# Layer one's first product of the first tile in four parts

## The chip, the cores and the metric

The kernel runs on one core of one Trainium2 chip. Five engines work side by side, each through its own list of instructions in order: TensorE (PE, with its weight loads as PEld), VectorE (DVE), ScalarE (ACT), GpSimd (POOL) and SyncE (SP), which starts the transfers that 16 DMA engines carry out. The metric is device time in microseconds (us), the median of three runs.

## The reference

Attention over 4 batches, 8 heads, 576 positions and 64 values per head; the first four heads see a window of 32 keys, the others every fourth key of a window of 128. Its output, 2304 rows of 512, goes through two layers.

```
scores = scale * np.matmul(q, k.transpose(0, 1, 3, 2))       # masked, softmax, times v
x = attn_out.transpose(0, 2, 1, 3).reshape(B * S, H * D)     # 2304 x 512

h = x @ w_in                                                 # layer one: 512 -> 1024
e = np.exp(h - np.max(h, axis=-1, keepdims=True))
solu = h * e / (np.sum(e, axis=-1, keepdims=True) + 1e-09)
ln = (solu - mean) / np.sqrt(var + 1e-06) * g_ln
y = ln @ w_out                                               # 1024 -> 512

h = y @ w2_in                                                # layer two: 512 -> 2048
out = (h * (1.0 / (1.0 + np.exp(-1.702 * h)))) @ w2_out      # 2048 -> 512
```

## The kernel before

**Three stages.** In the first some 280 us attention and layer one run interleaved, then layer two runs over three passes of 768 rows. A matmul of layer one takes each operand as a high and a low part: `x @ w` is `xh wh + xh wl + xl wh`.

**Attention units.** Each batch has five units: units 0 to 3 hold a pair of heads each with its first 512 queries, unit 4 the last 64 queries of all heads. A unit is a chain: scores on TensorE (tile `s`, line 271, after a mask that is added on TensorE at 267), row maximum on VectorE (`mx`, 306), exponential on ScalarE (`t`, 324 one window at a time, or 333 after VectorE's subtraction at 314), sums and reciprocal on VectorE (`sx`, 339 to 341), normalising on GpSimd or VectorE (346), transposition on TensorE (`ptp`, 354), copy (`pt`, 360), product with the values on TensorE (`xt`, 384 or 387: 64 matmuls in the trace), and two copies into the ring of rows `xr` (402, 406). `HPS = [0, 2, 1, 3]` says which pair of heads, and so which 128 of the 512 columns of a row (`kt`), a unit fills: units 1 and 3 fill columns `kt` 2 and 3, units 0 and 2 fill 0 and 1.

**Layer one.** A tile is 128 rows. `moe_xh` copies them from `xr` to `xh`, `moe_xl` makes `xl`, `moe_h` multiplies by one half of the 1024 columns of `w_in`: 4 `kt` by 3 products, 12 matmuls for a half, 24 for a tile.

**Weights.** `w_in` comes in four chunks as 64 bit words: chunk `c` holds `kt` 2(c mod 2) and the next, of the column half c // 2. Each is turned into float by two shifts (432 on ScalarE; 440 on ScalarE or 436 on VectorE), joined on VectorE (444), and split into `wi_h` (481) and `wi_l` (494).

**What sets the order.** Every step is a "work" with an engine. `ORDER`, a table of work numbers, gives the order in which all engines' instructions are written, `PICKS` the engine of the works that may run on several. Each engine runs its list in order and waits by semaphores for its operands and for free buffers. Where the planner's own reckoning shows a gap ahead of a TensorE work, `stir` writes up to four filler matmuls (line 253), which compute nothing that is used.

Of the kernel before, what the change touches and what calls it, by code (L numbers as in the profile page):

```python
# [9 lines left out]
F32R = mybir.dt.float32r  # L10
# [5 lines left out]
ALU = mybir.AluOpType  # L16
AX = mybir.AxisListType

P = 128
B, H, S, D = 4, 8, 576, 64  # L20
NT, DM, FF1, FF2 = 2304, 512, 1024, 2048
KT = DM // P
# [7 lines left out]
RING = 2 * S  # L30
# [135 lines left out]
def attention_moe_kernel(ctx, tc, qk, qk_last, v, v_last, masks, w_in, w_out, g_ln, w2_in, w2_out, out):  # L166
    nc = tc.nc
# [3 lines left out]
    def f32(ap):  # L171
        return ap.bitcast(F32)
# [332 lines left out]
    def moe_xh(i, copy):  # L505
        c0 = (i * P) % RING
        xh = hp_.tile([P, KT, P], F32R, tag="xh", bufs=2, name=f"xh{i}")
        copy(xh, xr[:, :, c0:c0 + P])
        xs[i] = [xh]

    def moe_xl(i, eng=nc.gpsimd):
        c0 = (i * P) % RING
        xl = hp_.tile([P, KT, P], F32R, tag="xl", bufs=2, name=f"xl{i}")
        eng.tensor_tensor(xl, xr[:, :, c0:c0 + P], f32(xs[i][0]), ALU.subtract)
        xs[i].append(xl)

    def moe_h(i, half):
        if half == 0:
            hps[i] = psA.tile([P, 2, 512], F32, tag="A", name=f"h{i}")
        stir(hps[i][:, half, :])  # L520
        xh, xl = xs[i]
        fs = slice(half * 512, half * 512 + 512)
        for kt in range(KT):
            for j, (x, w) in enumerate(((xh, wi_h), (xh, wi_l), (xl, wi_h))):
                nc.tensor.matmul(hps[i][:, half, :], x[:, kt, :], w[:, kt, fs],  # L525
                                 start=(kt == 0 and j == 0), stop=(kt == KT - 1 and j == 2))
# [422 lines left out]
    for i in range(NTILE):  # L949
# [5 lines left out]
        xh = add(r, "ACT", 0.63, lambda i=i: moe_xh(i, nc.scalar.copy), units, take=("x",), pick=0, port=True,  # L955
                 also=[("DVE", 0.42, lambda i=i: moe_xh(i, nc.vector.tensor_copy)),
                       ("POOL", 1.1, lambda i=i: moe_xh(i, nc.gpsimd.tensor_copy))])
        xl = add(r, "POOL", 1.3, lambda i=i: moe_xl(i), [xh], port=True,
                 also=[("DVE", 0.75, lambda i=i: moe_xl(i, nc.vector))] if i in XL_ANY else [])
        h0 = add(r, "PE", 2.8, lambda i=i: moe_h(i, 0), [xh, xl] + [w[c] for c in range(2) for w in (hi, lo)], take=("A",))  # L960
        h1 = add(r, "PE", 2.8, lambda i=i: moe_h(i, 1), [h0] + [w[c] for c in range(2, 4) for w in (hi, lo)], give=("x",))
# [324 lines left out]
def plan_sequence():  # L1286
# [29 lines left out]
    for b in range(1, B):  # L1316
        todo, k = items[b - 1], 0
        for u in range(UB):
# [30 lines left out]
XL_ANY = (0,)  # L1349
LO_POOL = (2,)  # L1350
# [15 lines left out]
ORDER = [1, 8, 56, 57, 58, 59, 18, 87, 88, 89, 0, 46, 60, 61, 4, 9, 77, 47, 48, 90, 49, 62, 50, 51, 78, 10, 97, 52, 7,  # L1366
# [243 lines left out]
```

## Time and profile before

| | |
|---|---|
| median of 3 runs | 651.91 us (651.39 to 652.36) |
| profiled execution | 652.14 us, span 650.4 us, mean granted clock 0.99 |
| TensorE busy | 631.7 us, 97% of the span, 5596 matmuls |
| VectorE, ScalarE, GpSimd busy | 436.1, 344.8, 265.7 us |
| moved by DMA | 163.53 MB, 251 GB/s in the mean |

The times come from one execution with a profiler. An engine's busy time over the span tells how much of the span it could be the limit; where it idles, the trace names what it waited for. A granted clock of 1 is TensorE's full 2.4 GHz, 0.5 is 1.2 GHz.

### The profile page before, as it was taken

How to read it: one execution, taken by the hardware profiler on the slowest of the kernel's cores; microseconds unless marked ns; L12 is line 12 of the kernel's file. 1: busy time of each engine (PE TensorE's matmuls, PEld its weight loads, DVE VectorE, ACT ScalarE, POOL GpSimd, SP SyncE). 2: the span in 40 equal slices, each digit the busy share in tenths (PEclk: the TensorE clock that was granted, in tenths of full speed). 3: DMA queues.
4: the chain of work that ended last, by engine and by line, in shares of the span. 5: the costliest groups of instructions: out<-in, count | busy, mean ns of one | idle time of the engine just before them, and what ended most of it. 6: DMA issues, size and time to landing. Idle time of an engine off the chain costs nothing.

```text
span 650.4 us, 14261 instructions
## 1 busy us (share of the span) xinstructions
PE 631.7 (97%) x5596; PEld 592.6 (91%) x5596; DVE 436.1 (67%) x773; ACT 344.8 (53%) x737; POOL 265.7 (41%) x331
## 2 busy tenths in 40 slices
PE   7599999999999999999999999999999999999997
PEld 4377888888989898999999999999999999999997
DVE  4689888475687566585778979433566854246784
ACT  4668976376444664754555765223265532235652
POOL 1317655836556766744365031202432340232232
PEclk9779999999999999999999999999999999999999
DMA  8959646643457547956999989776798957778783
GB/s 330 406 209 354 220 133 212 228 151 125 154 182 225 188 149 254 360 179 187 324 338 358 350 280 365 241 254 223 272 293 268 347 177 256 267 268 283 251 266 130
DMA packets 65011, 163.53 MB, mean 251 GB/s; under 512 B 6960, under 2 KB 28592, under 8 KB 64944
## 3 DMA queue, kind: packets, MB, share of 16 engines
q1 hardware_dynamic: 64944, 162.62, 73.4%
q8 instruction: 44, 0.72, 0.4%
q14 instruction: 23, 0.19, 0.1%
HBM read 126.42 MB, written 36.18 MB: 250 GB/s over the span
## 4 chain that ended last, share of the span: by engine, by line
PE 88%; DMA 7%; DVE 3%; POOL 1%; issue 1%; ACT 0%; SPq 0%; POOLq 0%; DVEq 0%; ACTq 0%
PE hz L720 15%; PE oz L798 15%; PE y L599 14%; PE h L525 14%; PE hx L720 12%; PE ox L798 11%; DMA w_t<-in_w_in_dram 3%; PE lt L579 2%; PE xt L387 1%; DMA wo<-wdo 1%; PE xt L384 1%; DMA y_early<-in_w_in_dram 1%; PE s L271 1%; DMA wdq<-park_hl 1%; PE ptp L354 1%; DMA qk<-in_qk_dram 1%
## 5 line engine op out<-in xcount | busy, mean ns | idle before, releaser
L763 ACT CAST gs<-g 128x384 fp32r<-128x384 f32 x168 | 84.1, 512 | 76.3 <-DVE g L759 27.3
L766 POOL TENSOR_TENSOR gs<-g,gs 128x384 fp32r<-128x384 f32 x47 | 49.9, 1067 | 144.1 <-ACT gs L763 136.0
L720 PE MATMUL hz<-yc,ws 128*128 128x384 f32 x492 | 98.5, 334 | 0.0
L599 PE MATMUL y<-ln_t,wo_h 128*128 128x384 f32 x384 | 98.5, 337 | 0.0
L766 DVE TENSOR_TENSOR gs<-g,gs 128x384 fp32r<-128x384 f32 x121 | 68.7, 590 | 28.1 <-ACT gs L763 26.3
L720 PEld LDWEIGHTS hz<-yc,ws 128*128 128x128 f32 x492 | 86.5, 188 | 0.0
L720 PE MATMUL hx<-yc,ws 128*128 128x384 f32 x369 | 74.7, 335 | 0.0
L599 PEld LDWEIGHTS y<-ln_t,wo_h 128*128 128x128 f32 x384 | 68.9, 188 | 0.5
L720 PEld LDWEIGHTS hx<-yc,ws 128*128 128x128 f32 x369 | 64.9, 188 | 0.0
L599 PE MATMUL y<-ln_t,wo_l 128*128 128x384 f32 x192 | 64.3, 335 | 0.0
L525 PE MATMUL h<-wi_h,xh 128*128 128x512 f32 x144 | 59.1, 410 | 0.5 <-DVE t L314 0.5
L798 PE MATMUL ox<-gs,wo 128*128 128x384 f32 x288 | 55.3, 337 | 1.4 <-DMA wo<-wdo 1.3
L525 PE MATMUL h<-wi_h,xl 128*128 128x512 f32 x144 | 56.5, 392 | 0.0
L525 PE MATMUL h<-wi_l,xh 128*128 128x512 f32 x144 | 56.3, 391 | 0.0
L798 PE MATMUL oz<-gs,wo 128*128 128x384 f32 x288 | 54.7, 336 | 0.0
L749 ACT ACTIVATE g<-g 128x384 f32<-128x384 f32 x72 | 36.4, 521 | 34.1 <-DVE g L742 13.1
L798 PE MATMUL oz<-gs,w 128*128 128x384 f32 x288 | 53.2, 337 | 0.0
L798 PEld LDWEIGHTS ox<-gs,wo 128*128 128x128 f32 x288 | 50.2, 188 | 2.2 <-DMA wo<-wdo 1.6
L798 PEld LDWEIGHTS oz<-gs,w 128*128 128x128 f32 x288 | 50.2, 188 | 0.4 <-DVE gs L766 0.4
L798 PEld LDWEIGHTS oz<-gs,wo 128*128 128x128 f32 x288 | 50.3, 188 | 0.1
L759 POOL TENSOR_TENSOR g<-g,g 128x384 f32<-128x384 f32 x21 | 22.8, 1089 | 66.4 <-ACT g L749 24.8
L759 DVE TENSOR_TENSOR g<-g,g 128x384 f32<-128x384 f32 x75 | 43.6, 597 | 7.6 <-POOL gs L766 5.8
(412 smaller groups left out, 1196.7 us busy)
## 6 DMA issues: line engine op xcount, KB each, us to landing
wo<-wdo SPq DMA_DIRECT2D x48, 512.0 KB, 6.0
ws<-wdq SPq DMA_DIRECT2D x41, 512.0 KB, 5.7
w<-wdo SPq DMA_DIRECT2D x72, 256.0 KB, 5.4
ws<-wdq SPq DMA_DIRECT2D x41, 384.0 KB, 4.8
qk<-in_qk_dram SPq DMA_DIRECT2D x14, 528.0 KB, 6.9
v<-in_v_dram SPq DMA_DIRECT2D x14, 512.0 KB, 6.8
out_dram<-ob SPq DMA_DIRECT2D x11, 384.0 KB, 5.9
w_t<-in_w_in_dram SPq DMA_DIRECT2D x8, 512.0 KB, 9.2
```

The lines of the kernel that those rows point to most:

```text
L271: nc.tensor.matmul(ps[QB * j:QB * j + QB, h, m * KW:m * KW + KW], q_[rows, c:c + QB], k_[rows, c:c + KW], start=not masked, stop=not maske ...
L354: nc.tensor.transpose(ps[:, j * P:j * P + P], t[:, 2 * j:2 * j + 2, :].rearrange("p m k -> p (m k)"), ident)
L384: nc.tensor.matmul(o, w, pt[rows, x:x + QB].rearrange("p (r t) -> p r t", r=4), start=True, stop=True, tile_position=(64 * par, 64 * h))
L525: nc.tensor.matmul(hps[i][:, half, :], x[:, kt, :], w[:, kt, fs], start=(kt == 0 and j == 0), stop=(kt == KT - 1 and j == 2))
L579: nc.tensor.transpose(ps[:, j, :], es[i][:, f * P:f * P + P], ident)
L599: nc.tensor.matmul(yps[g, dm][:, 0:TG].rearrange("p (t n) -> p t n", t=GT), w[:, f, ds_], x[:, :, f, :], start=(f == 0 and j == 0), stop=( ...
L720: nc.tensor.matmul(ps[:, 0:TB2], quad_weights(p, q, m, kk, a), yc2[m][:, x, kk, :], start=(m < 4 and kk == 0 and i == 0), stop=(kk == 1 an ...
L749: nc.scalar.activation(g_tile(q, 0, 0) if (half, b) == (0, 0) else src, src, AF.Gelu_apprx_sigmoid)
L759: eng.tensor_tensor(o_block(jj, *o), o_block(jj, *x), o_block(jj, *y_), op)
L763: nc.scalar.copy(gsp[jj, m][:, 0], o_block(jj, half, b))
L766: eng.tensor_tensor(gsp[jj, m][:, 1], o_block(jj, half, b), f32(gsp[jj, m][:, 0]), ALU.subtract)
L798: nc.tensor.matmul(ps, w, gsp[jj, m][:, x], start=m < 4 and first and i == 0, stop=last and i == 2, skip_group_check=True)
```

## The change

The product of tile 0 (`H_PARTS`) is made in four works in place of two: for `kt` 2 and 3 both column halves, then for `kt` 0 and 1 both column halves (`H_KTS`). Each has its own half of `xh` and `xl`, and waits for the two attention units and the one weight chunk that it reads in place of all four units and two chunks. The bank is opened by the first part (`start`) and closed by the last (`stop`). With the parts of `xh` and `xl` these are eight works in place of four, so the table has 2411 numbers in place of 2407, and the tables `ORDER` and `PICKS` are made anew for the whole program.

```diff
+    def moe_xh(i, copy, kts=range(KT)):
+        c0, k = (i * P) % RING, slice(kts[0], kts[-1] + 1)
+        if i not in xs:
+            xs[i] = [hp_.tile([P, KT, P], F32R, tag=f"x{z}", bufs=2, name=f"x{z}{i}") for z in "hl"]
+        copy(xs[i][0][:, k], xr[:, k, c0:c0 + P])
...
+    def moe_h(i, half, kts=range(KT)):
+        if i not in hps:
             hps[i] = psA.tile([P, 2, 512], F32, tag="A", name=f"h{i}")
-        stir(hps[i][:, half, :])
+        first, last = (0, KT - 1) if len(kts) == KT else (H_KTS[0][0], H_KTS[1][-1])
+        if kts[0] == first:
+            stir(hps[i][:, half, :])
...
-        for kt in range(KT):
+        for kt in kts:
             for j, (x, w) in enumerate(((xh, wi_h), (xh, wi_l), (xl, wi_h))):
                 nc.tensor.matmul(hps[i][:, half, :], x[:, kt, :], w[:, kt, fs],
-                                 start=(kt == 0 and j == 0), stop=(kt == KT - 1 and j == 2))
+                                 start=(kt == first and j == 0), stop=(kt == last and j == 2))
...
+        parts = H_KTS if i in H_PARTS else ()
+        for z, kts in enumerate(parts):
+            xh = add(r, "ACT", 0.38, lambda i=i, k=kts: moe_xh(i, nc.scalar.copy, k),
+                     [u for u, hp in zip(units, HPS) if hp in kts] + [xl], take=("x",)[z:], pick=0, port=True,
...
+            h0 = add(r, "PE", 1.4, lambda i=i, k=kts: moe_h(i, 0, k),
+                     [xl] + [w[kts[0] // 2] for w in (hi, lo)] + ([h0] if z else []), take=("A",)[z:])
+            h1 = add(r, "PE", 1.4, lambda i=i, k=kts: moe_h(i, 1, k),
+                     [h0] + [w[2 + kts[0] // 2] for w in (hi, lo)] + ([h1] if z else []), give=("x",)[:z])
...
+H_PARTS = (0,)
+H_KTS = ((2, 3), (0, 1))
...
-ORDER = [1, 8, 56, 57, 58, 59, 18, 87, 88, 89, 0, 46, 60, 61, 4, 9, 77, 47, 48, 90, 49, 62, 50, 51, 78, 10, 97, 52, 7,
```

TensorE, the start of tile 0's product, before: behind the transposition of unit 4 and the scores of unit 6 of the next batch (`s_646`) come 12 matmuls of the first column half (`h_695`), of which the first four rows and the last stand here.

```order
L354 MATMUL ptp_639<-ident,t_200 128x128 x2
...
L271 MATMUL s_646<-qk_597 32x64 x32
L253 LDWEIGHTS ident_b
L253 MATMUL h_695<-ident_b 128x512
L525 MATMUL h_695<-wi_h,xh_685 128x512
L525 MATMUL h_695<-wi_l,xh_685 128x512
...
L525 MATMUL h_695<-wi_h,xl_689 128x512
L384 MATMUL xt_0_725<-pt_691,vl_129 64x4x8
```

The same place in the changed program: unit 0's values product (`xt_0_592`), the transposition of unit 4, two fillers, 12 matmuls (six for each column half), then the values of unit 2 (`xt_0_687`).

```order
L384 MATMUL xt_1_593<-pt_457,v_476 64x4x8
L354 MATMUL ptp_633<-ident,t_247 128x128 x2
L253 LDWEIGHTS ident_b
L253 MATMUL h_652<-ident_b 128x512
...
L525 MATMUL h_652<-wi_h,xh_630 128x512
L525 MATMUL h_652<-wi_l,xh_630 128x512
...
L525 MATMUL h_652<-wi_h,xl_631 128x512
L253 LDWEIGHTS ident_b
L253 MATMUL xt_0_687<-ident_b 128x512
```

The product's first 12 matmuls now stand ahead of the values product of the fourth unit, and the other 12 behind it, a transposition, a score unit and unit 4's values.

VectorE around the rows' split of tile 0, before:

```order
L444 SCALAR_TENSOR_TENSOR w_t<-w_t 128x1024
L481 CAST wi_h<-w_t 128x2x512
L494 TENSOR_TENSOR wi_l<-w_t,wi_h 128x2x512 x2
L508 CAST xh_685<-xr 128x512
L514 TENSOR_TENSOR xl_689<-xr,xh_685 128x512
L306 TENSOR_REDUCE mx_693<-s_646 128x8
```

And in the changed program, from the low part of the second chunk to the last one:

```order
L494 TENSOR_TENSOR wi_l<-w_t,wi_h 128x2x512
L509 CAST xh_630<-xr 128x256
L306 TENSOR_REDUCE mx_636<-s_478 128x8
L513 TENSOR_TENSOR xl_631<-xr,xh_630 128x256
L436 TENSOR_SCALAR w_t<-w_t 128x1024
L444 SCALAR_TENSOR_TENSOR w_t<-w_t 128x1024
...
L444 SCALAR_TENSOR_TENSOR w_t<-w_t 128x1024 x2
L494 TENSOR_TENSOR wi_l<-w_t,wi_h 128x2x512
L513 TENSOR_TENSOR xl_631<-xr,xh_630 128x256
L494 TENSOR_TENSOR wi_l<-w_t,wi_h 128x2x512
```

The rows are split in two halves of 256 columns, with the conversion of the last two weight chunks between the halves. `s_478` is a score unit of the next batch.

SP, the loads of weights and values after the second weight chunk, before (`w_t` are chunks, two transfers each):

```order
L234 DMA y_early<-in_v_dram 128x1024
L425 DMA w_t<-in_w_in_dram 128x1024 x2
L234 DMA y_early<-in_v_dram 128x1024
L234 DMA v_530<-in_v_dram 128x1024
L425 DMA w_t<-in_w_in_dram 128x1024 x2
```

And in the changed program:

```order
L228 DMA qk_451<-in_qk_dram 128x1056
L234 DMA v_462<-in_v_dram 128x1024
L234 DMA v_476<-in_v_dram 128x1024
L425 DMA w_t<-in_w_in_dram 128x1024 x4
L425 DMA w_t<-in_w_out_dram 128x1024 x2
L234 DMA y_early<-in_v_dram 128x1024
```

The last two chunks of `w_in` now stand together, with the first chunk of `w_out` behind them and the values of one unit (`y_early`) behind that.

## Rows read from the trace of the kernel before

**Rows 1.** The page's engine line: busy us, share of the span, instructions.

```profile
PE 631.7 (97%) x5596; PEld 592.6 (91%) x5596; DVE 436.1 (67%) x773; ACT 344.8 (53%) x737; POOL 265.7 (41%) x331
```

**Rows 2.** Windows: us, busy of each engine, clock, DMA share, GB/s.

```profile
10.00:20.00 10.00, 5.19 (x178) 3.50 (x176) 6.87 (x15) 6.87 (x21) 1.35 (x2) 0.95 1.03 401
20.00:30.00 10.00, 7.49 (x173) 4.96 (x173) 5.28 (x10) 5.31 (x16) 2.70 (x2) 0.71 1.02 409
30.00:40.00 10.00, 8.00 (x206) 6.12 (x207) 7.87 (x13) 6.42 (x10) 2.08 (x2) 0.66 0.41 159
...
300.00:400.00 100.00, 98.58 (x567) 97.96 (x566) 80.32 (x151) 58.35 (x119) 35.54 (x42) 1.00 0.92 319
```

**Rows 3.** Timeline of TensorE from 0 to 36 us: start, us, engine, line, operation.

```profile
12.68 0.35 PE L271 MATMUL s<-y_early 64*32 64x64 f32 x16 [1.60 <-issue]
...
21.04 1.08 PE L384 MATMUL xt<-pt,v 64*64 64x32 f32 x31 [3.81 <-issue]
...
22.05 1.89 PE L253 MATMUL ptp<-ident_b 128*128 128x512 bf16 x4
...
27.28 0.88 PE L387 MATMUL xt<-pt,y_early 64*64 64x32 f32 x42 [0.60 <-issue]
...
31.43 0.66 PE L354 MATMUL ptp<-ident,t 128*128 128x128 f32 x4 [2.29 <-POOL t L346]
...
32.87 1.93 PE L384 MATMUL xt<-pt,y_early 64*64 64x32 f32 x64 [0.57 <-DVE pt L360]
```

**Rows 4.** Windows of TensorE between the ends of its stops.

```profile
12.60:21.00 8.40, 4.11 (x127) 0.88 1.03 406
21.00:27.20 6.20, 5.64 (x127) 0.61 1.03 408
```

**Rows 5.** DMA from 0 to 60 us: the queue of instructions; packets, MB, share.

```profile
q8 instruction: 8, 0.13, 0.8%
```

**Rows 6.** Timeline of TensorE from 39 to 54 us.

```profile
39.79 0.58 PE L525 MATMUL h<-wi_h,xh 128*128 128x512 f32 x1
...
44.53 0.50 PE L525 MATMUL h<-wi_h,xh 128*128 128x512 f32 x1
...
47.15 0.39 PE L525 MATMUL h<-wi_h,xl 128*128 128x512 f32 x1
...
47.70 0.86 PE L271 MATMUL s<-qk 64*32 64x64 f32 x64
...
48.49 1.09 PE L354 MATMUL ptp<-ident,t 128*128 128x128 f32 x8
...
50.76 0.47 PE L525 MATMUL h<-wi_h,xh 128*128 128x512 f32 x1 [0.49 <-DVE t L314]
```

**Rows 7.** Timeline of VectorE from 0 to 62 us.

```profile
32.73 1.22 DVE L444 SCALAR_TENSOR_TENSOR w_t<-w_t 128x1024 uint32<-128x1024 uint32 x1
...
34.71 2.36 DVE L494 TENSOR_TENSOR wi_l<-w_t,wi_h 128x1024 fp32r<-128x1024 f32 x2
36.98 0.42 DVE L508 CAST xh<-xr 128x512 fp32r<-128x512 f32 x1
37.44 0.69 DVE L514 TENSOR_TENSOR xl<-xr,xh 128x512 fp32r<-128x512 f32 x1
```

**Rows 8.** Timeline of ScalarE from 0 to 62 us.

```profile
10.90 1.75 ACT L324 ACTIVATE t<-s,mx 128x64 f32<-128x64 f32 x8
```

**Rows 9.** Chain of waits from 360 to 380 us: start, us, what.

```profile
369.64 7.84 DMA wo<-wdo
```

**Rows 10.** Windows of TensorE around the changes of its clock.

```profile
18.00:20.00 2.00, 0.00 (x0) 0.76 1.06 402
25.00:26.00 1.00, 1.00 (x66) 0.56 0.98 389
30.00:32.00 2.00, 0.57 (x5) 1.00 1.03 409
39.00:40.00 1.00, 1.00 (x66) 0.74 0.00 0
```

More of the change, by code (lines that the diff above doesn't have):

```diff
@@ L503, in attention_moe_kernel, with moe_xl @@
     lns, hps, es, xs, stat, sums = {}, {}, {}, {}, {}, {}
[L505 to L518, printed above, removed]
+    def moe_xh(i, copy, kts=range(KT)):
[3 more added lines that the diff above has]
+        copy(xs[i][0][:, k], xr[:, k, c0:c0 + P])
+    def moe_xl(i, eng=nc.gpsimd, kts=range(KT)):
+        c0, k = (i * P) % RING, slice(kts[0], kts[-1] + 1)
+        eng.tensor_tensor(xs[i][1][:, k], xr[:, k, c0:c0 + P], f32(xs[i][0][:, k]), ALU.subtract)
+    def moe_h(i, half, kts=range(KT)):
+        if i not in hps:
             hps[i] = psA.tile([P, 2, 512], F32, tag="A", name=f"h{i}")
-        stir(hps[i][:, half, :])
+        first, last = (0, KT - 1) if len(kts) == KT else (H_KTS[0][0], H_KTS[1][-1])
+        if kts[0] == first:
+            stir(hps[i][:, half, :])
         xh, xl = xs[i]
         fs = slice(half * 512, half * 512 + 512)
-        for kt in range(KT):
+        for kt in kts:
             for j, (x, w) in enumerate(((xh, wi_h), (xh, wi_l), (xl, wi_h))):
                 nc.tensor.matmul(hps[i][:, half, :], x[:, kt, :], w[:, kt, fs],
-                                 start=(kt == 0 and j == 0), stop=(kt == KT - 1 and j == 2))
+                                 start=(kt == first and j == 0), stop=(kt == last and j == 2))
     def h_flat(i):
@@ L954, in attention_moe_kernel @@
         r = at["h", i]
-        xh = add(r, "ACT", 0.63, lambda i=i: moe_xh(i, nc.scalar.copy), units, take=("x",), pick=0, port=True,
+        parts = H_KTS if i in H_PARTS else ()
+        xl = None
+        for z, kts in enumerate(parts):
+            xh = add(r, "ACT", 0.38, lambda i=i, k=kts: moe_xh(i, nc.scalar.copy, k),
+                     [u for u, hp in zip(units, HPS) if hp in kts] + [xl], take=("x",)[z:], pick=0, port=True,
+                     also=[("DVE", 0.29, lambda i=i, k=kts: moe_xh(i, nc.vector.tensor_copy, k)),
+                           ("POOL", 0.5, lambda i=i, k=kts: moe_xh(i, nc.gpsimd.tensor_copy, k))])
+            xl = add(r, "POOL", 0.75, lambda i=i, k=kts: moe_xl(i, nc.gpsimd, k), [xh], port=True,
+                     also=[("DVE", 0.42, lambda i=i, k=kts: moe_xl(i, nc.vector, k))])
+            h0 = add(r, "PE", 1.4, lambda i=i, k=kts: moe_h(i, 0, k),
+                     [xl] + [w[kts[0] // 2] for w in (hi, lo)] + ([h0] if z else []), take=("A",)[z:])
+            h1 = add(r, "PE", 1.4, lambda i=i, k=kts: moe_h(i, 1, k),
+                     [h0] + [w[2 + kts[0] // 2] for w in (hi, lo)] + ([h1] if z else []), give=("x",)[:z])
+        if parts:
+            h_of[i], xh_of[i] = h1, xl
+        xh = parts or add(r, "ACT", 0.63, lambda i=i: moe_xh(i, nc.scalar.copy), units, take=("x",), pick=0, port=True,
                  also=[("DVE", 0.42, lambda i=i: moe_xh(i, nc.vector.tensor_copy)),
                        ("POOL", 1.1, lambda i=i: moe_xh(i, nc.gpsimd.tensor_copy))])
-        xl = add(r, "POOL", 1.3, lambda i=i: moe_xl(i), [xh], port=True,
+        xl = xl or add(r, "POOL", 1.3, lambda i=i: moe_xl(i), [xh], port=True,
                  also=[("DVE", 0.75, lambda i=i: moe_xl(i, nc.vector))] if i in XL_ANY else [])
-        h0 = add(r, "PE", 2.8, lambda i=i: moe_h(i, 0), [xh, xl] + [w[c] for c in range(2) for w in (hi, lo)], take=("A",))
-        h1 = add(r, "PE", 2.8, lambda i=i: moe_h(i, 1), [h0] + [w[c] for c in range(2, 4) for w in (hi, lo)], give=("x",))
+        h0 = parts or add(r, "PE", 2.8, lambda i=i: moe_h(i, 0), [xh, xl] + [w[c] for c in range(2) for w in (hi, lo)], take=("A",))
+        h1 = h1 if parts else add(r, "PE", 2.8, lambda i=i: moe_h(i, 1), [h0] + [w[c] for c in range(2, 4) for w in (hi, lo)], give=("x",))
         h_of[i], xh_of[i] = h1, xl
@@ L1365 @@
 ULO_ANY = True
-ORDER = [1, 8, 56, 57, 58, 59, 18, 87, 88, 89, 0, 46, 60, 61, 4, 9, 77, 47, 48, 90, 49, 62, 50, 51, 78, 10, 97, 52, 7,
[123 rows of a table removed]
-PICKS = {50: 1, 52: 1, 54: 1, 55: 1, 73: 1, 86: 1, 91: 1, 104: 1, 127: 1, 136: 1, 146: 1, 159: 1, 160: 1, 168: 1,
[20 rows of a table removed]
+ORDER = [1, 4, 77, 78, 79, 18, 87, 88, 89, 0, 46, 47, 48, 80, 90, 8, 9, 267, 56, 266, 81, 82, 49, 50, 57, 58, 83, 59,
[123 rows of a table added]
+PICKS = {65: 1, 81: 1, 85: 1, 86: 1, 115: 1, 118: 1, 127: 1, 136: 1, 148: 1, 157: 1, 159: 1, 160: 1, 179: 1, 181: 1,
[20 rows of a table added]
 _INS = ["qk", "qk_last", "v", "v_last", "masks", "w_in", "w_out", "g_ln", "w2_in", "w2_out"]
```

286 rows, old and new, of tables (ORDER, PICKS) are left out of this document.

## The prediction

> **What bounds the kernel now.** I read the page's engine line first: TensorE is busy for 631.7 of 650.4 us [rows 1], so the whole reserve that any reordering can reach is 18.7 us of idle time, plus what a halved clock costs. The table by stretches says where that lies [rows 2]: between 10 and 40 us TensorE is busy for 5.19, 7.49 and 8.00 of 10 us each, at a mean granted clock of 0.95, 0.71 and 0.66 (1 is 2.4 GHz, 0.5 is 1.2); from 300 to 400 us it lacks 1.4 us; the stretches that are not shown lack little, except the last, where outputs are stored. From some 45 us on TensorE is the bound. What the change can win is therefore how much earlier TensorE has done the same work at about 50 us.
>
> Then the TensorE timeline of the start [rows 3]. Three of its stops are not waits for data: 1.60, 3.81 and 0.60 us "issue", each in the middle of a run of equal small matmuls. The trace tells what they are. From 12.6 us TensorE passes 127 matmuls, each with its weight load, up to the stop that ends at 21.04, and again 127 up to the stop that ends at 27.28 [rows 4]; and the queue of instructions moved 8 packets, 0.13 MB, in the first 60 us, 16 KB each [rows 5]. So TensorE's program comes in blocks of 127 matmuls with their loads, over the same transfer engines that carry the inputs; while these are full (a share of 1.03 in both stretches) one block came 8.36 us after the one before (12.68 to 21.04) and the next 6.24 us after that.
>
> The Trainium skill, "Runtime: NRT & Kernel Launch", section "Instruction fetch mechanics", also has a stream of 16 KiB blocks, but calls the cost of crossing one "mostly hidden". This trace does not agree for the start: 3.81 us at one crossing [rows 3]. By that rule the next crossing would cost nothing, and the two rivals below that rest on it would fall away; the forecast itself would stand, since VectorE then sets the same end. I count on the rows.
>
> The other stop is a true wait, 2.29 us for GpSimd's normalising at 31.43. Last, the product in question [rows 6]: its first matmul runs at 39.79, its last ends at 47.15 + 0.39 = 47.54 us, with the last unit's values and a score unit between its halves. The next tile's product starts at 50.76 after 0.49 us of waiting for VectorE.
>
> **The change part by part.** *The split itself.* The 24 matmuls stay 24: no weight load, no column is added. The splitting of the rows into high and low part becomes two instructions of half the size in place of one: for the whole tile VectorE took 0.42 and 0.69 us [rows 7]. Half the columns cost more than half of that and less than all of it; I take 0.3 and 0.42, so 0.3 us more in sum on VectorE and ScalarE. Its cover is TensorE's queue of values and scores; without cover it costs those 0.3 us.
>
> *The order.* The whole table was made anew, so I walk TensorE from block to block. Its first block edges fall at the same counts, and up to about 21 us the same transfers bound both programs (mask, one unit's queries and keys, the last unit, two more units, one weight chunk); I take the same ends, 12.68, 21.04 and 27.28. In the new order the edge at 27.28 lies in the scores of unit 7, and TensorE has one score unit more and one values product less behind it than before. Behind it come, at full clock, four fillers, a values product, a filler, a transposition and 12 matmuls of the next values product. Prices: a filler 0.24 (half of 1.89 / 4, a row at half clock), a values product 0.97 (half of 1.93), a transposition 0.55 (1.09 for two), [rows 3, 6]. That is 0.4 for the rest of the scores + 0.96 + 0.97 + 0.24 + 0.55 + 0.2 = 3.3 us, and about 0.4 us for ScalarE's eight exponentials (1.75 us, [rows 8]) and the copy behind them: TensorE stands at the next edge at 31.0. The block is there at 27.28 + 6.24 = 33.5. So the change takes out the wait for GpSimd (2.29) and puts 2.5 us of waiting for program code in its place.
>
> From 33.5 TensorE owes, up to the end of this product: the rest of the values product 0.8, half a transposition 0.27, two fillers 0.47, the first 12 matmuls 3.0 (44.53 to 47.54 for 12, [rows 6]), four fillers 0.94, the values of the fourth unit 0.97, a transposition 0.55, a score unit 1.2 (0.86, and some 0.3 for its mask between 47.15 and 47.70), two fillers 0.47, the last unit's values 0.5, and the last 12 matmuls 3.0. Together 12.2 us, so it ends at 45.7, against 47.54 before.
>
> *Are the operands there?* For the first 12: the last low part of the weights that they read (1.2) and half the rows follow the values product that ends near 30; with the next unit's maximum between them VectorE is through by 33.0, under the cover of the code wait. For the last 12 VectorE's queue decides. From 33.0 it holds two shifts of weight words that ScalarE did before, three joins (L444), the sums of one unit 1.1, a cast 0.69, two low parts and half the rows 0.42. A low part is 1.2 (two in 2.36) and a join 1.22 [rows 7]. The shift has no row in the start; the cast below it (0.69) and the join above it (1.22) bound it, and I take the cast, which likewise reads one operand. Sum 2 x 0.69 + 3 x 1.22 + 1.1 + 0.69 + 2.4 + 0.42 = 9.7: the last low part is ready at 42.7, just when TensorE comes to the last 12 (45.7 - 3.0). With the upper price it is 1.1 us late; were it cheaper than the cast nothing is won, since TensorE comes no sooner.
>
> *Up to the next tile.* Behind the product TensorE has a score unit, a values product and two transpositions, 3.4 us, to 49.1; VectorE, behind its row maximum (1.2) and the next unit's maximum and subtraction (0.69 each), lets the next product start at 49.2. That is 1.5 us before 50.76, with one transposition and one values product more done, and the last unit's scores of the next batch not yet (about 0.8): 0.55 + 0.97 - 0.8 = 0.7 us. Gain at that place: 1.56 + 0.7 = 2.3 us.
>
> *Afterwards.* The order has 38 fillers in place of 34; 27 against 25 of them by then, so two more later: 0.46 us. The 1.3 us that are lost near 376 us, where the chain has a 7.84 us load of weights [rows 9], I take as they are; the end has the same four last stores. Transfers: SP's queue has the same loads in another order, and the parked raw unit moved behind the weights, which costs TensorE nothing since its conversion is wanted only 100 us later.
>
> Sum: 2.3 - 0.46 = 1.85 us less. The profiled execution took 652.14 us with a span of 650.4; 652.14 - 1.85 = 650.3. The median of the three is 651.91, 0.23 below the profiled one, so 650.1 us is my forecast.
>
> **The rivals.** *The clock falls at the code wait.* It fell within 18 to 20 us, when TensorE had stood since 17.2 (mean 0.76 there), and had not come back before 25 to 26 us (mean 0.56), after 4.8 us of work; the second time the low level held to within 39 to 40 us (mean 0.74), some 6.6 us from 32.9 [rows 10]. The 2.29 us stop before 31.43 alone did not bring it down (1.00 from 30 to 32 us), nor did the 1.60 us stop. If 2.5 us at 31.0 do, TensorE works at 1.2 in place of 2.4 GHz for 4.8 to 6.6 us and loses 2.4 to 3.3 us: a time 0.6 to 1.4 us above before, 652.8.
>
> *The block comes as late as the one at 21.04.* One mechanism on the other side: with 8.36 in place of 6.24 us, which TensorE's third block took under full transfer engines, it stands at unit 0's values product until 35.6, 4.6 us, longer than the 3.81 us stop that brought the clock down. The price is 2.1 us more than the rival above: 654.9. With the clock down it makes the kernel slower by more than 0.2% from a block at 33.9 on. For it: four weight transfers now stand in one row in SP's queue ahead of that time. Against it: the later of the two blocks seen took 6.24, and from 30 to 40 us the share before was down to 0.41 [rows 2].
>
> *Given back later.* The stage at 376 us is fed by transfers that are busy for 0.92 of 300 to 400 us [rows 2]; if the load that ends at 377.5 comes when it came, the gain goes there: 651.9. Against it: that queue waits mostly for buffers that TensorE frees, which move with it.
>
> *It does not do what it says.* The first half runs early, but what is late is the last half, which still wants all rows and weights: if VectorE's two shifts cost the upper 1.22 and a further join lands ahead of the last low part, the product ends near 47.5 as before: 651.9.
>
> **How the numbers follow.** Forecast 0.48 (650.1); clock falls 0.20 (652.8); given back 0.05 and not late 0.05 (651.9 both); late block 0.22 (654.9). What this measurement can tell from no change is 0.2%, 1.3 us: faster means below 650.6, slower above 653.2. The forecast alone is faster, 0.48; clock, giving back and not late are the same, 0.30; the late block is slower, 0.22. The range goes from 647.6 to 654.2: its low end is the forecast without the 1.4 us of idle time from 300 to 400 us and with 1.1 us more, if the block and VectorE's queue are both that much sooner than I took them; its high end leaves out half of the late block's. The forecast's own range is 649.0 to 651.2, by the price of the shift (2 x 0.53 us) to either side.
>
> **What would show it.** The trace after should have an "issue" stop near 33 us in a values product of 64 matmuls, no wait for GpSimd near 31, twelve h matmuls before 40 us, the last of the 24 ending near 45.7, and the next tile's first h matmul near 49.2. A granted clock of 0.5 from 33 to 39 means the first rival; a stop that ends after 33.9, the second. The forecast is wrong in its core if the 24 matmuls end after 47 us at full clock, or if TensorE idles more than 3 us between 50 and 640.

## The result, and the profile after

| | before | after |
|---|---|---|
| median | 651.09 us (13 runs, 647.88 to 653.73) | 654.26 us (13 runs, 651.07 to 660.52) |
| ratio after / before | | 1.0061, 95% interval 1.0036 to 1.0085 |
| profiled execution | 652.14 us, span 650.4 | 655.89 us, span 654.0 |

The change makes the kernel 0.6% slower. The profiled executions lie 1.05 and 1.63 us above their medians. Forecast was 650.1 us; the measured time lies just above the range (647.6 to 654.2). Ratios, here and below, are to runs of the kernel before on the same chip in the same batch, with disturbed runs left out, so they need not follow the medians to the last tenth.

The page's engine line after, busy time first, answers to [rows 1]:

```profile
PE 634.3 (97%) x5600; PEld 593.5 (91%) x5600; DVE 441.3 (67%) x791; ACT 341.9 (52%) x730; POOL 247.9 (38%) x322
```

2.6 us more of TensorE's time (four fillers more are in it) in a span that is 3.6 us longer. The table by stretches after, against [rows 2]; the columns are TensorE, its weight loads, VectorE, ScalarE, GpSimd, granted clock, DMA share, GB/s:

```profile
10.00:20.00 10.00, 7.41 (x246) 4.57 (x245) 7.40 (x16) 8.07 (x24) 1.04 (x1) 1.00 1.01 370
...
20.00:30.00 10.00, 6.65 (x170) 4.78 (x170) 6.93 (x16) 5.47 (x14) 3.00 (x3) 0.61 1.02 405
...
30.00:40.00 10.00, 8.98 (x158) 6.19 (x156) 6.88 (x13) 6.25 (x16) 2.36 (x3) 0.88 0.89 306
...
50.00:60.00 10.00, 7.72 (x114) 6.01 (x107) 9.11 (x17) 7.91 (x13) 4.58 (x9) 0.83 1.00 381
...
300.00:400.00 100.00, 97.93 (x559) 96.37 (x558) 77.54 (x152) 58.90 (x116) 38.69 (x43) 1.00 0.93 316
```

From 30 to 40 us TensorE now does 8.98 us at a clock of 0.88, where it did 8.00 at 0.66: the early half of the product is there. But from 20 to 30 us it lost 0.84 us, and from 50 to 60 us it has 7.72 us at 0.83, where it was busy for 9.07 at full clock. The stops of the start, TensorE's timeline after (start, length, what, and in brackets the idle time ahead with what ended it), against [rows 3]:

```profile
6.83 1.18 PE L271 MATMUL s<-y_early 64*32 64x64 f32 x64 [2.81 <-DMA y_early<-in_qk_dram]
...
14.22 0.34 PE L271 MATMUL s<-qk 64*32 64x64 f32 x15 [1.05 <-issue]
...
22.30 0.68 PE L271 MATMUL s<-qk 64*32 64x64 f32 x32 [3.46 <-issue]
...
29.14 0.90 PE L271 MATMUL s<-qk 64*32 64x64 f32 x41 [1.05 <-issue]
...
35.34 1.00 PE L384 MATMUL xt<-pt,v 64*64 64x32 f32 x51 [1.02 <-issue]
```

The first scores start at 6.83 us, not at 4.93, after 2.81 us of waiting for a transfer into `y_early`, and each block edge ends later than before: 14.22, 22.30, 29.14 against 12.68, 21.04, 27.28. The instruction queue moved as much as before [rows 5]:

```profile
q8 instruction: 8, 0.13, 0.8%
```

Then the product itself and what follows it, against [rows 6]:

```profile
36.79 0.58 PE L525 MATMUL h<-wi_h,xh 128*128 128x512 f32 x1
...
45.25 0.50 PE L525 MATMUL h<-wi_h,xh 128*128 128x512 f32 x1
...
47.88 0.39 PE L525 MATMUL h<-wi_h,xl 128*128 128x512 f32 x1
...
52.13 0.33 PE L354 MATMUL ptp<-ident,t 128*128 128x128 f32 x1 [1.46 <-POOL t L346]
...
53.28 1.76 PE L354 MATMUL ptp<-ident,t 128*128 128x128 f32 x7 [0.82 <-issue]
...
54.69 0.78 PE L525 MATMUL h<-wi_h,xh 128*128 128x512 f32 x1
```

The first half runs from 36.79 us, the second from 45.25 and ends at 47.88 + 0.39 = 48.27 us (before 47.54). Between it and the next tile's first matmul, at 54.69 (before 50.76), stand two stops, 1.46 us for GpSimd's normalising and 0.82 us at a block edge, and the clock is at half for what comes next (0.63 for a matmul that else takes 0.39). VectorE's timeline over the same time, against [rows 7]:

```profile
35.88 0.69 DVE L436 TENSOR_SCALAR w_t<-w_t 128x1024 uint32<-128x1024 uint32 x1
...
39.42 1.54 DVE L436 TENSOR_SCALAR w_t<-w_t 128x1024 uint32<-128x1024 uint32 x1
...
44.85 1.22 DVE L494 TENSOR_TENSOR wi_l<-w_t,wi_h 128x1024 fp32r<-128x1024 f32 x1
...
47.38 2.44 DVE L498 SCALAR_TENSOR_TENSOR wo_l<-w_t,g_sb,wo_h 128x512 fp32r<-128x512 f32 x2
...
49.75 0.67 DVE L339 TENSOR_REDUCE sx<-t 128x8 f32<-128x512 f32 x1
...
52.59 0.69 DVE L314 TENSOR_TENSOR t<-s,mx 128x512 f32<-128x512 f32 x1
```

Its two shifts took 0.69 and 1.54 us, and ahead of unit 8's sums (49.75), on which the normalising waits, stands the low part of a chunk of the second weight matrix, 2.44 us at 47.38. At the first product of layer two the changed kernel is 2.31 us behind, which at the end of the span has become 3.6:

```profile
277.71 1.29 PE L720 MATMUL hx<-yc,ws 128*128 128x384 f32 x6
```

(before)

```profile
280.02 1.31 PE L720 MATMUL hx<-yc,ws 128*128 128x384 f32 x6
```

(after)

The clock does not carry the difference of the medians: span times (1 - mean granted clock), averaged over the runs, is 7.0 us after and 6.6 before (the 33 runs beside e1 to e4); span times clock is 645.7 and 642.5. The 3.2 us are time in which TensorE stood, did more, or ran slower than the granted clock says (e6's trace below has such a stretch), not a lower granted clock.

### The profile page after: what moved, and what is told of

The parts are those of the page before. It is cut to its first block, busy times and chain, and to the rows that moved or that the text cites. A ratio compares the mean times of both kernels' runs of the same rounds, so it can differ in the third digit from the quotient of the medians.

```text
span 654.0 us, 14242 instructions
## 1 busy us (share of the span) xinstructions
PE 634.3 (97%) x5600; PEld 593.5 (91%) x5600; DVE 441.3 (67%) x791; ACT 341.9 (52%) x730; POOL 247.9 (38%) x322
## 4 chain that ended last, share of the span: by engine, by line
PE 89%; DMA 5%; DVE 3%; issue 1%; POOL 0%; ACT 0%; SPq 0%; POOLq 0%; DVEq 0%
PE y L599 15%; PE hz L720 15%; PE h L525 15%; PE oz L798 14%; PE hx L720 11%; PE ox L798 9%; PE lt L579 3%; PE s L271 2%; PE xt L387 2%; DMA wo<-wdo 1%; PE ptp L354 1%; DMA wdo<-hl_('o', 3, 1)_1_5004 1%; PE xt L384 1%; DMA wdo<-hl_('o', 3, 0)_0_4800 1%; DMA y_early<-in_qk_dram 1%
## 5 line engine op out<-in xcount | busy, mean ns | idle before, releaser
L766 DVE TENSOR_TENSOR gs<-g,gs 128x384 fp32r<-128x384 f32 x133 | 73.9, 576 | 27.6 <-ACT gs L763 27.3
L766 POOL TENSOR_TENSOR gs<-g,gs 128x384 fp32r<-128x384 f32 x35 | 37.1, 1062 | 141.3 <-ACT gs L763 127.1
```

The costliest lines, as they stand in the source:

```text
L766: eng.tensor_tensor(gsp[jj, m][:, 1], o_block(jj, half, b), f32(gsp[jj, m][:, 0]), ALU.subtract)
```

## The experiments

Theory after the result: the loss has two places, the first load (unit 3's queries and keys, now the first that TensorE needs, come in two transfers: units 2 and 3 of the first batch have lent buffers, parts of another tile, and the code loads such a unit's queries and keys separately) and VectorE's queue behind the product. Rivals: the split itself; the pace of the blocks of program code; the clock.

A trace shows one execution. Up to 60 us e1 and e16 are the same program, and so are after and e17, before and e18; between such traces a block edge moves by up to 2.8 us and the next tile's start by 0.7 to 1.6 us. A difference of that size between two traces shows nothing by itself.

**e1, one transfer for a lent unit.**

```diff
-            nc.sync.dma_start(q_, qk[idx][:, 0:nq])
-            nc.sync.dma_start(k_, qk[idx][:, nq:])
+            both_ = flat[:, nl * (idx - 2):nl * (idx - 2) + nq + nk]
+            nc.sync.dma_start(both_, qk[idx])
```

> The changed kernel, but the queries and keys of a unit whose buffer is lent come in one transfer (528 KB) in place of two (256 and 272 KB). Theory: the two transfers are why the first scores start at 6.83 us in place of 4.93; with one, the first scores start near 4.9, every later stop of TensorE ends 1.5 to 1.9 us earlier (14.22, 22.30, 29.14, 35.34 become about 12.6, 20.7, 27.3, 33.6) and the kernel takes 1.9 us less than the changed one: about 652.3. Rival: the blocks of program code set TensorE's pace from 14 to 36 us, whatever the first scores do; then the first scores come earlier, the stops end within 0.5 us of where they did, and the time stays at 654.3 (within 0.5).

650.47 us, ratio 1.0003 (0.9980 to 1.0026), so its interval lies below that of the changed kernel: 3.8 us less, twice what was expected. That is the time of before, not less. Its timeline of TensorE:

```profile
4.93 1.18 PE L271 MATMUL s<-y_early 64*32 64x64 f32 x64 [0.92 <-DMA y_early<-in_qk_dram]
...
12.57 0.34 PE L271 MATMUL s<-qk 64*32 64x64 f32 x15 [1.69 <-issue]
...
18.77 0.58 PE L271 MATMUL s<-qk 64*32 64x64 f32 x31 [1.87 <-issue]
...
25.07 0.90 PE L271 MATMUL s<-qk 64*32 64x64 f32 x40 [0.60 <-issue]
...
48.40 0.33 PE L354 MATMUL ptp<-ident,t 128*128 128x128 f32 x1 [1.45 <-POOL t L346]
...
49.70 0.76 PE L525 MATMUL h<-wi_h,xh 128*128 128x512 f32 x1
```

The first scores are at 4.93 as forecast, and the next edges end not 1.5 to 1.9 but 1.7, 3.5 and 4.1 us sooner than after. (In e16 it is 0.4, 1.2 and 1.7: 13.85, 21.14 and 27.44.) The stop at 48.40 is GpSimd's again; the next tile starts at 49.70. Why the load in two is late shows in the line of its second part after, beside the line of the loads of as many bytes in one transfer before (the shortest of each line is the first load):

```profile
L225 SPq DMA_DIRECT2D y_early<-in_qk_dram x2: 334/379/424, 1.6 to 6.7; - x2
...
DMA to landing us min/median/max: 5.1/7.1/9.1
```

(after, line 225)

```profile
L228 SPq DMA_DIRECT2D qk<-in_qk_dram x14: 327/328/3923, 1.2 to 140.1; - x14
...
DMA to landing us min/median/max: 3.7/6.9/10.2
```

(before, line 228)

The one transfer lands 3.7 us after its issue; of the two, the second lands 5.1 us after its own issue, and that is 0.47 us later than the first's (1.64 against 1.17).

**e2, e3, the low part put later (alone, and with e1).** The edit moves work 290 in `ORDER` from behind unit 8's subtraction to behind the next tile's weighting:

```diff
-  ... 130, 131, 93, 104, 289, 290, 94, 95, ... 283, 291, 345, 29, 140, ...
+  ... 130, 131, 93, 104, 289, 94, 95, ... 283, 291, 345, 290, 29, 140, ...
```

> The changed kernel, but the low part of the first chunk of the second weight matrix (two instructions, 2.44 us on VectorE at 47.38) stands behind the next tile's weighting in VectorE's order instead of ahead of the sums of unit 8. Theory: it is what makes the stop before 52.13 (1.46 us for GpSimd's normalising, 0.82 us issue) and with it the fall of the clock at 53; without it the next tile's first h matmul starts near 52.2 in place of 54.69, TensorE keeps full clock from 50 to 60 us (0.83 before the edit), and the time falls by 2.4 to 3.5 us, to about 651.3. Rival: the stop is set by the exponentials and by GpSimd, or by program code (the 0.82 us issue); then the first h matmul of the next tile stays within 0.7 us of 54.69 and the time within 1 us of 654.3.

> Both edits of the two runs beside it. Theory: the two losses add, since one shifts the whole start and the other lies behind it: 4.3 to 5.4 us less than the changed kernel, about 649.5, 1 to 2 us below the kernel before. Rival: whatever is won before 50 us is given back at the next code block or the next load, and the time stays at or above that of the better single edit.

e2: 656.03 us, 1.0075 (1.0047 to 1.0102); e3: 654.01, 1.0051 (1.0030 to 1.0071). The theory of VectorE's queue fell: in place of a gain of 2.4 us, e3 is slower than e1 by 3.5. Two of e2's stops and the start of the next tile show why e2 gains nothing:

```profile
52.74 1.26 PE L354 MATMUL ptp<-ident,t 128*128 128x128 f32 x6 [1.53 <-issue]
...
53.86 0.99 PE L525 MATMUL h<-wi_h,xh 128*128 128x512 f32 x1
...
76.45 0.44 PE L354 MATMUL ptp<-ident,t 128*128 128x128 f32 x2 [0.66 <-POOL t L346]
```

GpSimd's wait was gone, and the block edge stood in its place, 1.53 us: the next tile started 0.8 us sooner, not 2.5. And what was put off came due at 76 us, as a wait of 0.66 us for a normalising whose sums stood behind the moved work. What makes e3's median 3.5 us worse than e1's is not shown: its trace is of its shortest run (651.10), and there the next tile starts at 50.16 and layer two at 276.53, both some 0.5 us after e1.

**e4, the split alone,** in the order of before: the second parts (305 to 308) stand right behind the first ones, and the numbers behind them are raised by four.

```diff
-  ... 66, 301, 302, 92, ... 280, 303, 121, ... 718, 304, 96, ...
+  ... 66, 301, 302, 305, 306, 92, ... 280, 303, 307, 121, ... 722, 304, 308, 96, ...
```

> The order of the kernel before, with only the product of the first tile split in four parts that stand where the two halves stood (and the high and low part of its rows in two pieces each, where the one piece stood). Theory: the split costs 0.3 us on VectorE beside TensorE's other work and decides nothing: 651.1, within 0.7 us of the kernel before. Rival: the split itself is the loss (smaller pieces, more dependencies): 2 to 3 us above before, 653 to 654.

650.20 us, 0.9991 (0.9973 to 1.0010). The split costs nothing, and by itself brings nothing that can be measured.

**e5, e6, e9, which of the loads, and which property of them.** e5 joins unit 3's load alone, e9 unit 2's alone; e6 keeps two transfers, each of 64 whole rows:

```diff
+            for c0, c1 in ((0, nq + nk),) if idx == 3 else ((0, nq), (nq, nq + nk)):   # e9: idx == 2
+                nc.sync.dma_start(flat[:, nl * (idx - 2) + c0:nl * (idx - 2) + c1], qk[idx][:, c0:c1])
```
```diff
+            for p0 in (0, 64):                                                        # e6
+                nc.sync.dma_start(flat[p0:p0 + 64, nl * (idx - 2):nl * (idx - 2) + nq + nk], qk[idx][p0:p0 + 64])
```

> The changed kernel, with only the unit that TensorE scores first (unit 3) loaded in one transfer; the other lent unit keeps its two. Theory: this one transfer is the whole difference; first scores at 4.9 us, stops that end near 12.6, 18.8, 25.0 and 31.1, time 650.5 (within 0.8), as with both units in one transfer (650.47). Rival: the second lent unit's two transfers, issued at 5.6 and 6.7 us, crowd the block of code that TensorE waits for at 22.30; then the first scores are at 4.9 but the second stop still ends near 20.5 to 21, and the time is 652 to 653.

> The changed kernel, with each lent unit still loaded in two transfers, but halved by partitions (64 rows of 4,224 bytes each) and not by columns (128 rows of 2,048 and of 2,176 bytes). Theory: what makes the load late is that its rows come in packets half as long, whose rest is served among the packets of the transfers behind it (the last ones from 4 to 6 us); with whole rows the first scores are at 5.0 to 5.3 us and the time near 650.5 to 651.2. Rival: two transfers are late because they are two, whatever their rows; then the first scores stay at 6.2 to 6.9 us and the time at 653 to 654.5.

> The changed kernel, with only the second lent unit (unit 2) loaded in one transfer; unit 3, which TensorE scores first, keeps its two. Joining unit 3's alone gave 653.29, joining both 650.47. Theory: each has its own effect, unit 3's on the first scores and unit 2's on the wait for the second block of code (from the crossing at the first stop to the transfer of the block 5.5 to 6.7 us where unit 2 comes in two column parts, 3.8 to 4.2 where not); so the first scores stay at 6.8, the first stop ends near 14.2, the second near 20.4 in place of 22.30, and the time is 651.5 to 652.5. Rival: unit 2's transfers are all of it; then 650.5. Other rival: neither alone does anything, the two only together; then 654.

e5 653.29 us, 1.0045 (1.0021 to 1.0069); e6 653.12, 1.0025 (1.0001 to 1.0049); e9 653.15, 1.0031 (0.9998 to 1.0063). In e5 the first scores are early and the second edge is not (first two rows), in e9 neither is (next two):

```profile
4.79 1.19 PE L271 MATMUL s<-y_early 64*32 64x64 f32 x64 [0.77 <-DMA y_early<-in_qk_dram]
...
22.20 0.68 PE L271 MATMUL s<-qk 64*32 64x64 f32 x31 [4.43 <-issue]
```

```profile
6.57 1.17 PE L271 MATMUL s<-y_early 64*32 64x64 f32 x64 [2.56 <-DMA y_early<-in_qk_dram]
...
21.80 0.46 PE L271 MATMUL s<-qk 64*32 64x64 f32 x31 [3.17 <-issue]
```

So in e5 the 1.9 us of the first scores are swallowed by the next block of code, and e1's gain needed both: neither load alone accounts for it, and e9's own expectation failed (21.80, not 20.4). More traces bear this out (e9's is of its longest run). With the fillers and the four parts as after, the second edge ends at 18.8 to 21.1 us and the next tile starts at 48.9 to 50.8 in the four with both loads joined (e1, e3, e8, e16); it is 21.8 to 22.5 and 53.9 to 56.6 in the five with one or none (after, e2, e5, e9, e17). In e6 the scores start at 4.82, then stand for the second half of the rows:

```profile
4.82 0.42 PE L271 MATMUL s<-y_early 64*32 64x64 f32 x2 [0.81 <-DMA y_early<-in_qk_dram]
...
6.03 1.17 PE L271 MATMUL s<-y_early 64*32 64x64 f32 x62 [0.79 <-DMA y_early<-in_qk_dram]
```

The bulk starts at 6.03, between e1's 4.93 and the 6.83 after. But this trace cannot say what its time is made of. Its next tile starts at 51.02 and layer two at 276.00, as early as in e1 (275.97); the span is 653.9 because TensorE slows down later. From 370 to 408 us its matmuls of 384 columns start 0.200 us apart in place of 0.173, which makes some 5 us. From 370 to 400 it does 151 (first row), in e1 175 (second), without a stop and at a granted clock of 1.00 in both:

```profile
370.00:400.00 30.00, 30.00 (x151) 1.00 0.92 315
```

```profile
370.00:400.00 30.00, 30.00 (x175) 1.00 0.99 331
```

No other trace here has such a stretch, and why this one has it is not known. So whether e6's median comes from the number of transfers, and whether the short rows count, stays open.

**e7, e8, looking for a better version.** e7 is e4 with e1's edit; e8 is e1 with work 290 behind 185, where VectorE waited for TensorE.

> The order of the kernel before with the product split in place, and the lent units in one transfer each. Theory: there unit 3 is the fifth load and is scored from 10.36 us, 2 us after it has landed, so that joining its two transfers moves no scores; the joined loads shorten only the crowd of packets ahead of the second block of code: 649.5 to 650.4 (650.2 with the split alone). Rival: the pace of the code blocks hangs on how many transfers are queued; then the second block comes up to 2 us sooner (a stop that ends near 19.5 in place of 21.5) and the time is 648 to 649.

> One transfer per lent unit, and the low part of the first w_out chunk (2.43 us on VectorE at 43.67) put where VectorE waited 1.48 us for the next tile's product (behind the maximum of unit 13, before 58.06). Theory: behind the next tile's weighting it cost 2 us or more because VectorE has no idle time from 58 to 80 us; in the gap about 1.5 of its 2.4 us are free, and the stop for GpSimd before 48.40 (1.45) goes, though the block of code that TensorE needs there bounds the gain to about 0.5: 649.8 to 650.5. Rival: any delay of VectorE's queue behind 50 us comes out at the end in full; then 651.5 to 653.

e7 650.03 us, 0.9980 (0.9957 to 1.0002); e8 651.89, 1.0012 (0.9986 to 1.0039). e7's second edge stayed where e4's was (21.60 against 21.51), so the rival of e7 fell: in the order of before joining the loads changes nothing that can be told. e8 spread from 648 to 660 and decides nothing.

**e10, the pace of the code, by more of it.** e1 with each filler in four:

```diff
-            nc.tensor.matmul(bank.rearrange("p (o n) -> p o n", o=4), ident_b, x, start=True, stop=True)
+            for o in range(4):
+                nc.tensor.matmul(bank[:, o * P:o * P + P], ident_b, ident_b, start=True, stop=True)
```

> One transfer per lent unit (650.47), and each filler matmul of 512 columns written as four of 128 columns: the same columns on TensorE, three matmuls with their weight loads more per filler, 42 more by the third block edge and 57 more by the fourth. Theory: TensorE's pace up to 31 us is that of the blocks of code (127 matmuls with their loads, at least 6.1 us from edge to edge); 57 more are 0.45 of a block, so the first matmul of the product comes 2 to 3 us later than 32.54 and the kernel takes 1.5 to 3 us more: 652 to 653.5. Rival: the stops called issue are waits for data or for transfers that the code does not govern; then the product starts within 0.5 us of where it did and the time within 0.7 of 650.5.

653.07 us, 1.0029 (1.0005 to 1.0053), 2.6 above e1 (1.7 by the ratios, whose intervals overlap). TensorE's edges and the first matmul of the product:

```profile
21.18 0.85 PE L272 MATMUL s<-qk 64*32 64x64 f32 x64 [3.68 <-issue]
...
27.21 1.04 PE L254 MATMUL ptp<-ident_b 128*128 128x128 bf16 x8 [3.77 <-issue]
...
36.59 0.48 PE L526 MATMUL h<-wi_h,xh 128*128 128x512 f32 x1
```

The product starts 4 us later than in e1 (32.54) although TensorE has the same columns to do, and its stops called issue up to there are 4.0 us longer (8.65 against 4.63). But of the other traces with e1's start, e16 has it at 35.35 after 8.13 us of such stops. That more instructions cost waiting for their code fits this; the size, 1.2 to 4.1 us, is not settled.

**e11, the early half.** e1 with the product in two halves where the last two parts stood (`H_PARTS = ()`, works 301 to 304 taken out of `ORDER`).

> One transfer per lent unit (650.47), the changed kernel's order, but the product of the first tile in two halves again: both halves and the rows' high and low part stand where the last two of the four parts stood, nothing of the product runs near 32 us. Theory: this undoes the gain that the four parts were made for: 12 matmuls (2.8 us) move from the stretch at 32.5 to 35.6 us to behind the last weights at 41.5; what TensorE waits for there hides some, and the next tile's first matmul comes 1 to 2.5 us later: 651.5 to 653. Rival: VectorE's and GpSimd's work sets the next tile's start (49.7) in any case, so that the early matmuls only fill a wait: 650.5 within 0.6.

651.81 us, 0.9997 (0.9970 to 1.0025), not told apart from e1. In the trace the next tile starts at 51.89 against 49.70 and layer two at 277.67 against 275.97, as the theory had it, but over the runs the worth of the four parts can't be told from nothing: the medians are 1.3 us apart, and the ratios lie the other way.

**e12 to e18, the fillers.** e12 is e1 without any filler, e13 the changed kernel, e14 the kernel before and e15 e7 without any; e16 is e1 without those behind 60 us, e17 and e18 the changed kernel and the one before likewise.

```diff
-STIR = 7
+STIR = 0
-            self.gap = w.gap
+            self.gap = w.gap if w.start < 60 else 0.0     # e16 to e18, with STIR = 7
```

> One transfer per lent unit (650.47), and no filler matmul at all (28 fewer up to 48 us, 38 in all). Theory of the blocks: 28 matmuls are 0.22 of a block, so the stops for code shrink by up to 1.4 us: 649 to 650. Rival: the fillers hold the clock; without them it is down for longer (more than the 10 to 12 us seen between 18 and 53 us) and the time is 651.5 to 653.

> The changed kernel as it is (two transfers per lent unit), without fillers. Theory: the late first load costs its 3.8 us whether fillers are there or not; the fillers cost 2.4 us behind 60 us (10 of 0.235) and some 0.5 before: 651.4, within 1 us. Rival: the loss is the pace of the code blocks, which fillers lengthen; then without them most of the loss is gone and the time is 648 to 649.5.

> The kernel before, without its 34 fillers (8 of them behind 60 us). Theory: 8 x 0.235 = 1.9 us less behind 60 us, and 0.5 in the start: 648.2 to 649 against 650.6. Rival: in the old order the fillers hold the clock through the stops at 18 to 21 and 29 to 31 us; without them it is lower for longer, and the time is 650 to 652.

> The old order with the product split in place and the lent units in one transfer each (650.03), without fillers. Theory: the same 2.4 us less as in the other kernels: 647.6, within 0.8, level with the changed order under the same edits (647.57), so that neither order is better than the other. Rival: the changed order uses the time that the fillers gave up better, since its 12 early matmuls stand ready; then this one stays at 649 or above.

> One transfer per lent unit (650.47), fillers kept up to the 28th and left out behind 60 us (10). Theory: behind 60 us TensorE is the bound and each filler costs its 0.235 us: 2.35 us less, 648.1, so that most of the gain without fillers (2.9) is here. Rival: the gain lies in the start (fewer matmuls per block of code, and fillers that run late into the data they wait beside); then 649.8 to 650.5.

> The changed kernel, only its 10 fillers behind 60 us left out (all 38: 649.66). Theory: these cost 10 x 0.235 = 2.35 us, the 28 of the start the other 2.2: 651.9, within 0.8. Rival: nearly all of the 4.6 us is behind 60 us, as in the joined kernel (647.41 against 647.57 without any): 649.5 to 650.5.

> The kernel before, only its 8 fillers behind 60 us left out (all 34: 650.92, no gain). Theory: these cost 8 x 0.235 = 1.9 us here too and the 26 of the start give back as much, by the clock that they hold: 649.1, within 0.7. Rival: in the old order TensorE waits behind 60 us for other reasons and the fillers there cost nothing: 650.9.

| | fillers kept | behind 60 us out | all out |
|---|---|---|---|
| before | 651.09 | e18 650.84, 1.0009 (0.9989 to 1.0028) | e14 650.92, 1.0010 (0.9985 to 1.0035) |
| after | 654.26, 1.0061 (1.0036 to 1.0085) | e17 653.35, 1.0052 (1.0024 to 1.0079) | e13 649.66, 0.9975 (0.9956 to 0.9993) |
| after, loads joined (e1) | 650.47, 1.0003 (0.9980 to 1.0026) | e16 647.41, 0.9935 (0.9912 to 0.9959) | e12 647.57, 0.9935 (0.9911 to 0.9959) |
| before's order, split, loads joined (e7) | 650.03, 0.9980 (0.9957 to 1.0002) | | e15 650.07, 0.9979 (0.9956 to 1.0002) |

e12 and e17 lie outside both of their ranges, e14, e15 and e18 went with their rivals. In the changed kernel all the fillers cost 4.6 us by the medians (5.6 by the ratios), those of the start some 3.7 (5.0) of it (e13 against e17): the rival of e13 is the nearer. In the order of before they cost nothing on balance. The averages over the runs say what they do: without them span times (1 - clock) rises from 7.0 to 9.2 us after and from 6.6 to 8.7 before, so they save some 2 us of lost clock in either; but span times clock falls from 645.7 to 638.7 after (standard error 0.7) and only from 642.5 to 641.4 before (1.5). In e7 and e15, before's order too, both move by more and cancel (5.3 to 9.8; 642.9 to 638.6, standard error 1.6). That in the changed kernel the fillers cost what they do because they are instructions in a start that waits for its instructions is argued from e10 and from e13's trace, and not shown. In e13's profile the edges end at 21.62, 27.91 and 34.33 in place of 22.30, 29.14 and 35.34, and the next tile starts 3.8 us sooner than after, of which 1.0 is there at the fourth edge; behind it e13 has no stop at an edge before that tile:

```profile
21.62 0.64 PE L271 MATMUL s<-qk 64*32 64x64 f32 x21 [2.63 <-issue]
...
27.91 0.66 PE L271 MATMUL s<-qk 64*32 64x64 f32 x27 [1.52 <-issue]
...
34.33 1.08 PE L384 MATMUL xt<-pt,v 64*64 64x32 f32 x33 [1.85 <-issue]
...
50.93 0.47 PE L525 MATMUL h<-wi_h,xh 128*128 128x512 f32 x1 [0.20 <-DVE t L314]
```

With the loads joined the fillers of the start make no difference (e12 against e16): the gain over e1 lies behind 60 us. So the two remedies of the start, joined loads and no fillers, do not add.

e12 and e16 beat both kernels, by 0.65% of before. That e16 gains 3.1 us where the fillers left out take 2.35, and the same edit nothing in e18, is not explained; e16 has 6 runs. In its trace layer two starts 2.25 us sooner than in e1 (275.97), though its next tile started 1.11 later (50.81): between the two it is 3.4 us quicker, also more than the ten take:

```profile
273.72 1.31 PE L720 MATMUL hx<-yc,ws 128*128 128x384 f32 x6
```

## Why the prediction was wrong, step by step

- **The split itself** costs nothing: right (e4). The halves cost 0.42 for the low part, as taken, and 0.29 to 0.41 for the high one.
- **"Up to about 21 us the same transfers bound both programs"**: the step that failed first. Its sentence named the same set of loads; their order differs, and the first one is in two parts. TensorE's third edge ended at 29.14, not 27.28: 1.86 us. With the loads joined, and nothing else touched, 3.8 us of the loss are gone. The forecast gain is not there even so: it was 1.85 us, a ratio of 0.9972, and e1's is 1.0003 (0.9980 to 1.0026). That e1's 650.47 lies near the 650.1 is luck, since that was counted from 651.91 and before's median over 13 runs is 651.09; and so it is with e1's next tile, 49.70 where 49.2 was forecast: its fourth edge ended 2.4 us sooner than forecast (31.10 against 33.5), and from there it took 2.9 us longer (18.6 against 15.7).
- **The pace of the blocks** was right: 35.34 - 29.14 = 6.20 us, taken as 6.24. So was the place of the stop, in a values product of 64 matmuls, and that the wait for GpSimd near 31 us goes. The stop itself was 1.02 us and not 2.5, because TensorE was at half clock for most of the way to it (a mean of 0.61 from 20 to 30 us); the sum had counted the way at full clock.
- **From the edge to the end of the product**: 12.2 us forecast, 12.93 measured (35.34 to 48.27).
- **VectorE's last low part**: 42.7 forecast, 46.07 measured. 1.86 of it are inherited, 0.85 the second shift (1.54, above the upper bound of 1.22). The sum had it due for the first of the last 12 matmuls, at 45.25; none of the 12 waited, so it did not stop TensorE.
- **From the product to the next tile**, the other step that failed: 3.5 us forecast, 6.42 measured, and 5.15 in e1 (44.55 to 49.70). The sum counted a row maximum, a maximum and a subtraction on VectorE and left out the 2.44 us low part of the second matrix and unit 8's sums ahead of them. That was not the binding term, though: with the low part out of the way (e2) the block edge holds TensorE there all the same. The sum had no stop at an edge behind the fourth; there is one, 383 matmuls on, at 53.28.
- Together 1.84 + 0.73 + 2.92 = 5.5 us at 54.69 against 49.2, and the profiled execution took 655.89 against 650.3, 5.6 more. That the two agree is partly luck: from the next tile to layer two the changed program took 1.6 us less than before (225.33 against 226.95), and from there to the end 1.3 us more.
- **Afterwards**: the waits for weights from 300 to 400 us grew from 1.3 to 2.0 us, where none was forecast to change.
- **The rivals.** The clock at the code wait: no, 0.88 from 30 to 40 us, above before. The late block: the stop ended after 33.9 as its mark said, but the block came 6.20 us after the last, so the mechanism is another. Given back at 376 us: there was no gain to give back, and the waits there grew by 0.7 us. It does not do what it says: the product did end late (48.27) and one shift did cost more than 1.22, but by the edges, not by VectorE, which stopped none of its matmuls.
- **Not settled**: the wait from the first stop's end to the transfer of the next block. It is 3.8 to 5.3 us in the seven runs of the changed order with both lent loads joined, 4.2 in e6 (halved by rows), and 5.0 to 6.7 in the twelve others. That joining both shortens it there, and with it the second edge, is seen; why joining one does not, nor both in the old order, is not shown.

## What to carry to other kernels

Where a new order brings another transfer to the front, look at that transfer's own form, not only at the set of loads: one that lands in two parts is ready when the second part is. While inputs fill the transfer engines, instructions can have a price of their own, also those that compute nothing. Before a wait is taken away, find what stands right behind it: here a wait for an engine hid a wait for code. And before a trace is set against a trace, see how far two traces of one program lie apart: here up to 2.8 us at one edge.

## What the runs showed of the hardware

TensorE's code came in step with its edges. After, the eight 16 KB packets of the instruction queue in the first 60 us started 0.8 to 5.7 us after TensorE crossed one edge (11.79 us for the crossing at 8.91, 19.91 for 14.22, 50.91 for 48.45), and the five stops at a next edge ended 2.4 to 2.6 us after such a start (14.22, 22.30, 29.14, 35.34, 53.28). Up to 36 us, where the transfer engines were full for most of the time (shares of 1.01, 1.02 and 0.89 after), there were 6.0 to 9.1 us between stops at neighbouring edges, over all runs. The Trainium skill, "Runtime: NRT & Kernel Launch", section "Instruction fetch mechanics", calls the cost of such a crossing "mostly hidden". Here it was not: every run has at least two stops at edges up to 36 us, the longest of 4.62 us (e17), though some crossings show none (e7's third).
